# Moving tiles of the full blocks read as two halves by turns, with a matching change of token order in the stores

## Chip, cores, metric

One core of one Trainium2 chip runs the whole program. The metric is device time in microseconds, median of the runs. TensorE (PE) multiplies, VectorE (DVE), ScalarE (ACT) and GpSimd (POOL) work element by element, and SyncE (SP) issues the transfers.

## The reference, cut to what matters

```python
def mab(q, kv):                                  # attention, scale = 1 / sqrt(128)
    s = scale * (q @ kv.T); a = softmax(s); return a @ kv
h = mab(inducing, x)                             # 32 x 128 from 12480 tokens x 128
x = mab(x, h)                                    # 12480 x 128
def _moe_ref(x, w_in, w_out, s, b):              # d_ff = 2048
    r = np.maximum(x @ w_in, 0.0)
    return (s * (r * r) + b) @ w_out
def _moe2_ref(x, w_in, w_out):
    h = x @ w_in
    g = np.where(h >= 1, h, np.where(h <= -1, 0.0, (h + 1) ** 2 / 4))
    return g @ w_out
```

The inputs are float32, the weight matrices float64. The output is 12480 x 128 float32.

## The kernel before

The tokens are worked in 25 blocks: 24 full ones of 512 tokens (`TB`) and a short one of 192. Tokens lie along the free dimension, the 128 channels on the partitions. A first part reads `x`, transposes it into tiles `x0` to `x24`, computes the 32 x 128 attention result, and turns the float64 weights into float32 (`win`, `wo_s`) or into two halves, a rounded one and the rest (`half(name, 0)`, `half(name, 1)`).

Then two feed-forward layers run as one software pipeline. One step handles two of the 16 chunks of `d_ff` (`GW` = 2, `SPB` = 8 steps a block, 200 steps in all). Of step t, layer 1 does `in1` (product of the softmax weights `qt` with `hw`, two matmuls), `relu1`, `sq1`, `split1` and, two steps later, `out1`; layer 2 works `LAG` = 18 steps behind with `in2`, `clip2`, `sq2`, `g2`, `split2_hi`, `split2_lo` and, three steps later, `out2`. To keep precision at the speed of one pass, `in2`, `out1` and `out2` are each three matmuls per chunk: (rounded weight, rounded data), (rounded weight, rest of data), (rest of weight, rounded data), all of type F32R. With a full block each reads a moving tile of 128 x 512 four-byte words and writes one bank of 128 x 512 in PSUM. A steady step holds 2 + 6 + 6 + 6 = 20 of these one-pass matmuls. In the first 18 steps the product of layer 1 is `out1_whole`, plain float32, which the trace shows as two MATMUL records for one matmul; the last, short block ends with `out2_whole`, float32 too.

The order on each engine is fixed by the code: a planner (`Plan`) with estimated costs orders the first part, the first steps and the last ones, and the string `ORDER` the steps between: `in1 relu1 ev1 sq1 evh out2 in2 ev2 clip2 hi2- lo2- misc sq2 evl miscd split1 out1 g2`, where the minus means the step before. Layer 1 has one buffer for `h1` (two banks of PSUM), layer 2 two for `h2`; `y1` and `y2` are one bank each. So `in2` of a step waits for `lo2` of two steps before, which is the last reader of its buffer.

`store(bl)` reads the accumulated `y2` bank: DVE transposes it in 32 x 32 squares into a tile `o` (two buffers), and four transfers, one for each group of 32 channels, write it to the output in pieces of 32 floats. A block's tokens were loaded four to a partition, so column k*128 + p of a tile is token 4p + k, and the store's address pattern undoes that.

In the trace before, L661 is `in1`; L714, L715 and L716 are the three matmuls of `outp` (for `out1` and `out2` alike); L726 is `out1_whole`; L751 to L753 are `in2`; L795 is `out2_whole`; L758, L762, L769, L235 and L779 are `clip2`, `sq2`, `g2`, `split2_hi` and `split2_lo`; L674 and L681 `relu1` and `sq1`; L691 and L239 `split1`.

## Time and profile before

| what | value |
|---|---|
| three runs | 983.13, 985.3, 987.97 us, median 985.3 |
| the profiled execution | 984.17 us, of which the span (first to last instruction) is 982.4 us |
| PE busy | 959.7 us, 98% of the span |
| DVE, ACT, POOL busy | 805.0, 843.6, 753.3 us |
| granted TensorE clock, mean | 0.995 |
| DMA | 28.11 MB, most of it in the first 60 us |

The page gives busy times by engine, the span in 40 slices, the chain of work that ended last, and the costliest groups of instructions. A MATMUL's duration in it includes the time to drain, and the ends are modelled; the time that a stream of matmuls needs is therefore read from one start to the next in the timeline.

### The profile page before, as it was taken

The numbers are of one execution on the slowest core, as the hardware profiler recorded it, in microseconds if no ns is written. First come the engines' busy times: TensorE is split into PE (matmuls) and PEld (weight loads), VectorE is DVE, ScalarE is ACT, GpSimd is POOL, SyncE is SP. The second block draws the span as 40 slices with busy tenths as digits, with TensorE's granted clock in tenths as the row PEclk, the third lists the DMA queues.
The fourth block names the chain that finished last, engine by engine and source line by source line (L and its number), as shares of the span: only waits on it lengthen the run. The fifth ranks groups of instructions, "written<-read, shape, count | busy, mean of one in ns | idle before, by whom it ended". The sixth has DMA issues, their size and how long they took to land.

```text
span 982.4 us, 12391 instructions
## 1 busy us (share of the span) xinstructions
PE 959.7 (98%) x4492; PEld 770.0 (78%) x4492; DVE 805.0 (82%) x834; ACT 843.6 (86%) x910; POOL 753.3 (77%) x510
## 2 busy tenths in 40 slices
PE   5999999999999999999999999999999999999997
PEld 3754588888888888888888888888888888888776
DVE  6878788888888878888888888878888888888895
ACT  5748989989898988998898898998998899898774
POOL 0121379988899888899889898888898888887463
PEclk9989999999999999999999999999999999999999
DMA  8612000100002000002000002000001000000000
GB/s 322 218 31 78 0 1 12 44 11 12 4 7 54 11 1 12 11 0 54 12 1 11 11 0 55 12 1 11 11 1 43 12 1 11 16 1 11 11 12 15
DMA packets 65469, 28.11 MB, mean 29 GB/s; under 512 B 54016, under 2 KB 58368, under 8 KB 65408
## 3 DMA queue, kind: packets, MB, share of 16 engines
q1 hardware_dynamic: 65408, 27.33, 10.5%
q8 instruction: 35, 0.57, 0.2%
q14 instruction: 26, 0.21, 0.1%
HBM read 14.80 MB, written 6.39 MB: 22 GB/s over the span
## 4 chain that ended last, share of the span: by engine, by line
PE 93%; ACT 2%; DVE 2%; DMA 2%; issue 0%; DVEq 0%; ACTq 0%
PE y L714 17%; PE y L715 17%; PE y L716 17%; PE h L751 9%; PE h L753 9%; PE h L752 9%; PE h L661 9%; PE y L726 3%; DMA xc<-in_x_dram 1%; PE ptr L305 1%; DVE cl L758 1%; ACT g L681 1%; PE ph L378 1%; ACT g L674 1%; DVE lo L779 1%; PE pw L883 1%
## 5 line engine op out<-in xcount | busy, mean ns | idle before, releaser
L691 POOL TENSOR_TENSOR lo<-g,hi 128x1024 fp32r<-128x1024 f32 (+1 forms) x182 | 427.7, 2350 | 15.2
L758 DVE TENSOR_SCALAR cl<-h 128x1024 f32<-128x1024 f32 (+2 forms) x202 | 239.3, 1186 | 126.0 <-PE h L753 125.9
L762 ACT ACTIVATE cl<-cl,mhalf 128x1024 f32<-128x1024 f32 (+2 forms) x202 | 226.8, 1124 | 83.9 <-DVE cl L758 83.6
L714 PE MATMUL y<-hi,wout 128*128 128x512 f32 (+1 forms) x748 | 289.5, 387 | 0.9 <-DVE o L804 0.9
L715 PE MATMUL y<-lo,wout 128*128 128x512 f32 (+1 forms) x748 | 289.3, 387 | 0.0
L716 PE MATMUL y<-hi,wout 128*128 128x512 f32 (+1 forms) x748 | 289.2, 387 | 0.0
L239 POOL TENSOR_SCALAR hi<-g 128x1024 fp32r<-128x1024 f32 (+1 forms) x182 | 187.0, 1027 | 88.8 <-PE y L716 75.7
L769 DVE SCALAR_TENSOR_TENSOR h<-h,cl 128x1024 f32<-128x1024 f32 x182 | 223.2, 1226 | 13.9 <-ACT cl L762 2.7
L779 DVE TENSOR_TENSOR lo<-h,hi 128x1024 fp32r<-128x1024 f32 x182 | 221.6, 1217 | 3.0 <-ACT hi L235 0.5
L681 ACT ACTIVATE g<-g 128x1024 f32<-128x1024 f32 (+1 forms) x200 | 207.5, 1039 | 5.4
L674 ACT ACTIVATE g<-h 128x1024 f32<-128x1024 f32 (+1 forms) x197 | 194.2, 986 | 5.3 <-PE h L661 5.3
L235 ACT CAST hi<-h 128x1024 fp32r<-128x1024 f32 x182 | 181.7, 999 | 4.8 <-DVE h L769 4.8
L714 PEld LDWEIGHTS y<-hi,wout 128*128 128x128 f32 x748 | 140.5, 188 | 29.8 <-issue 1.3
L716 PEld LDWEIGHTS y<-hi,wout 128*128 128x128 f32 x748 | 140.4, 188 | 28.7
L715 PEld LDWEIGHTS y<-lo,wout 128*128 128x128 f32 x748 | 140.5, 188 | 28.3
L751 PE MATMUL h<-y,win 128*128 128x512 f32 (+1 forms) x400 | 154.8, 387 | 1.1 <-DVE lo L779 1.0
L752 PE MATMUL h<-y,win 128*128 128x512 f32 (+1 forms) x400 | 153.9, 385 | 0.0
L753 PE MATMUL h<-y,win 128*128 128x512 f32 (+1 forms) x400 | 153.8, 385 | 0.0
L661 PE MATMUL h<-qt,hw 128*128 128x512 f32 (+1 forms) x400 | 124.9, 396 | 0.7 <-ACT g L674 0.6
L661 PEld LDWEIGHTS h<-qt,hw 128*128 128x128 f32 x400 | 74.5, 188 | 22.8 <-issue 6.2
L751 PEld LDWEIGHTS h<-y,win 128*128 128x128 f32 x400 | 75.1, 188 | 17.8 <-DVE lo L779 2.0
L753 PEld LDWEIGHTS h<-y,win 128*128 128x128 f32 x400 | 75.2, 188 | 15.1
(139 smaller groups left out, 612.5 us busy)
## 6 DMA issues: line engine op xcount, KB each, us to landing
xc<-in_x_dram SPq DMA_DIRECT2D x24, 256.0 KB, 6.5
out_dram<-o SPq DMA_DIRECT2D x96, 64.0 KB, 2.2
qin<-x SPq DMA_DIRECT2D x92, 64.0 KB, 2.0
raw_in<-in_moe_w_in_dram SPq DMA_DIRECT2D x8, 512.0 KB, 5.6
raw_out<-in_moe_w_out_dram SPq DMA_DIRECT2D x8, 512.0 KB, 6.2
xc<-in_x_dram SPq DMA_DIRECT2D x1, 96.0 KB, 6.7
qin<-x SPq DMA_DIRECT2D x4, 24.0 KB, 2.7
out_dram<-o SPq DMA_DIRECT2D x4, 24.0 KB, 1.9
```

The source lines that it names most:

```text
L661: nc.tensor.matmul(p[:, j, :tb(bl)], hw[f // 4][:, (f % 4) * 128:(f % 4 + 1) * 128], qt[bl], start=True, stop=True)
L691: engine[eng].tensor_sub(lo1[t], g1.pop(t), hi1[t].bitcast(F32))
L714: nc.tensor.matmul(p, whi, hi[:, j, :], start=first, stop=False)
L715: nc.tensor.matmul(p, whi, lo[:, j, :], start=False, stop=False)
L716: nc.tensor.matmul(p, wlo, hi[:, j, :], start=False, stop=last)
L751: nc.tensor.matmul(p[:, j, :tb(bl)], whi, y1h[bl], start=True, stop=False)
L752: nc.tensor.matmul(p[:, j, :tb(bl)], wlo, y1h[bl], start=False, stop=False)
L753: nc.tensor.matmul(p[:, j, :tb(bl)], whi, y1l[bl], start=False, stop=True)
L758: nc.vector.tensor_scalar(cl[t][:, part(js)], h2[t][:, part(js), :tb(t // SPB)], -1.0, 1.0, op0=ALU.max, op1=ALU.min)
L762: nc.scalar.activation(k, k, AF.Square, bias=mhalf, scale=0.5)
L769: nc.vector.scalar_tensor_tensor(oo[t][:, part(js)], h, -1.0, cl[t][:, part(js)], op0=ALU.max, op1=ALU.add)
L779: engine[eng].tensor_sub(lo2[t][:, part(js)], oo[t][:, part(js)], hi2[t][:, part(js)].bitcast(F32))
```

## The change

Two helpers make views of a tile of a full block. `turns` reads it in the order 0, 256, 1, 257, ..., 255, 511: the first and the second half by turns, so neighbouring columns come from addresses 1024 bytes apart and each half is walked in sequence. `turned` describes the output with two inner elements that follow each other, so that the product's columns are written to PSUM in plain sequence. Column 2b + a of the output is thus token column 256a + b of the input.

This is done in `in1`, `outp` (`out1` and `out2`), `out1_whole` and `in2` for the 24 full blocks. The element-wise work between is unchanged: it does not mind which token a column is. Each of the four products on a token's way rotates the nine bits of the column number by one, four in all, and with the order from loading the store needs another address pattern. It is still four transfers a block, of 64 KB each, in pieces of 32 floats. The short block keeps its order; `out2_whole`, which serves it alone, is untouched. Neither the planner's costs nor the order of instructions on any engine changes: the two programs stand in the same order on PE, DVE, ACT, POOL and SP, and the only rows that differ in shape are the stores (outermost count 8 in place of 128).

```diff
+    def turns(v, bl):
+        return v.rearrange("p (a b) -> p b a", a=2) if tb(bl) == TB else v
+    def turned(v, bl):
+        return v.rearrange("p (b a) -> p b a", a=2) if tb(bl) == TB else v
...
-            nc.tensor.matmul(p[:, j, :tb(bl)], hw[f // 4][:, (f % 4) * 128:(f % 4 + 1) * 128], qt[bl],
-                             start=True, stop=True)
+            nc.tensor.matmul(turned(p[:, j, :tb(bl)], bl), hw[f // 4][:, (f % 4) * 128:(f % 4 + 1) * 128],
+                             turns(qt[bl], bl), start=True, stop=True)
...
-        p = p[:, :tb(t // SPB)]
+        bl = t // SPB
+        p = turned(p[:, :tb(bl)], bl)
         for j in js:
+            mhi, mlo = turns(hi[:, j, :], bl), turns(lo[:, j, :], bl)
...
-            nc.tensor.matmul(p, whi, hi[:, j, :], start=first, stop=False)
-            nc.tensor.matmul(p, whi, lo[:, j, :], start=False, stop=False)
-            nc.tensor.matmul(p, wlo, hi[:, j, :], start=False, stop=last)
+            nc.tensor.matmul(p, whi, mhi, start=first, stop=False)
+            nc.tensor.matmul(p, whi, mlo, start=False, stop=False)
+            nc.tensor.matmul(p, wlo, mhi, start=False, stop=last)
...
-            nc.tensor.matmul(acc1(bl)[:, :tb(bl)], wo_s[:, f, :], g[:, j, :], ...
+            nc.tensor.matmul(turned(acc1(bl)[:, :tb(bl)], bl), wo_s[:, f, :], turns(g[:, j, :], bl), ...
...
-            nc.tensor.matmul(p[:, j, :tb(bl)], whi, y1h[bl], start=True, stop=False)
-            nc.tensor.matmul(p[:, j, :tb(bl)], wlo, y1h[bl], start=False, stop=False)
-            nc.tensor.matmul(p[:, j, :tb(bl)], whi, y1l[bl], start=False, stop=True)
+            o, mhi, mlo = turned(p[:, j, :tb(bl)], bl), turns(y1h[bl], bl), turns(y1l[bl], bl)
+            nc.tensor.matmul(o, whi, mhi, start=True, stop=False)
+            nc.tensor.matmul(o, wlo, mhi, start=False, stop=False)
+            nc.tensor.matmul(o, whi, mlo, start=False, stop=True)
...
-        ov = out[t0:t0 + n].rearrange("(q t k) (r d) -> r t k q d", t=NM, k=kb, d=NM)
+        if n == TB:
+            ov = out[t0:t0 + n].rearrange("(q s u) (r d) -> r u q s d", q=KB, u=2 * KB, d=NM)
+        else:
+            ov = out[t0:t0 + n].rearrange("(q t k) (r d) -> r t k q d", t=NM, k=kb, d=NM)
+            o = o.rearrange("p (k q) d -> p k q d", k=kb)
         for r in range(C // NM):
-            nc.sync.dma_start(out=ov[r], in_=o[NM * r:NM * (r + 1)].rearrange("p (k q) d -> p k q d", k=kb))
+            nc.sync.dma_start(out=ov[r], in_=o[NM * r:NM * (r + 1)])
```

## Rows read from the trace of the kernel before

**Rows 1.** The page: busy us, share and instructions; then the chain that ended last.

```profile
PE 959.7 (98%) x4492; PEld 770.0 (78%) x4492; DVE 805.0 (82%) x834; ACT 843.6 (86%) x910; POOL 753.3 (77%) x510
PE 93%; ACT 2%; DVE 2%; DMA 2%; issue 0%; DVEq 0%; ACTq 0%
```

**Rows 2.** Windows: stretch, busy us (instructions) of PE, PEld, DVE, ACT, POOL; clock, DMA.

```profile
60.00:130.00 70.00, 68.02 (x250) 35.51 (x248) 56.74 (x86) 58.37 (x66) 21.05 (x18) 1.00 0.14 38
...
567.00:676.00 109.00, 109.00 (x482) 90.26 (x481) 90.36 (x81) 98.84 (x101) 95.66 (x63) 1.00 0.08 18
...
894.00:950.00 56.00, 54.95 (x268) 44.88 (x266) 49.73 (x43) 42.66 (x51) 31.26 (x30) 1.00 0.03 6
950.00:983.00 33.00, 26.26 (x147) 22.87 (x146) 21.32 (x33) 16.06 (x20) 15.50 (x7) 0.95 0.11 20
```

**Rows 3.** Timeline of PE in a steady step: start, length, instruction.

```profile
500.16 0.62 PE L661 MATMUL h<-qt,hw 128*128 128x512 f32 x2
500.61 0.39 PE L714 MATMUL y<-hi,wout 128*128 128x512 f32 x1
...
504.69 0.61 PE L661 MATMUL h<-qt,hw 128*128 128x512 f32 x2
```

**Rows 4.** Groups of PE by line and shape, the whole span: counts and mean.

```profile
L714 PE MATMUL y<-hi,wout 128*128 128x512 f32 x732 | 285.3, 390 | 0.9 <-DVE o L804 0.9
L751 PE MATMUL h<-y,win 128*128 128x512 f32 x384 | 150.1, 391 | 1.1 <-DVE lo L779 1.0
L661 PE MATMUL h<-qt,hw 128*128 128x512 f32 x384 | 122.0, 401 | 0.7 <-ACT g L674 0.6
L726 PE MATMUL y<-g,wo_s 128*128 128x512 f32 x72 | 33.9, 607 | 1.2 <-ACT g L681 0.7 <-ACT y1f L730 0.4
```

**Rows 5.** Timeline of PE: plain float32 records, of 512 and of 192 columns.

```profile
79.15 4.03 PE L726 MATMUL y<-g,wo_s 128*128 128x512 f32 x9
...
969.50 1.46 PE L795 MATMUL y<-g,x 128*128 128x192 f32 x8
```

**Rows 6.** Timeline of PE after a short product has broken the stream.

```profile
903.46 0.36 PE L661 MATMUL h<-qt,hw 128*128 128x192 f32 x2
903.66 0.42 PE L714 MATMUL y<-hi,wout 128*128 128x512 f32 x1
903.92 0.40 PE L715 MATMUL y<-lo,wout 128*128 128x512 f32 x1
904.16 0.39 PE L716 MATMUL y<-hi,wout 128*128 128x512 f32 x1
...
905.77 0.40 PE L751 MATMUL h<-y,win 128*128 128x512 f32 x1
```

**Rows 7.** Timeline of PE: one-pass products of 192 columns, the first with weights ready.

```profile
961.98 0.25 PE L751 MATMUL h<-y,win 128*128 128x192 f32 x1
962.06 0.28 PE L752 MATMUL h<-y,win 128*128 128x192 f32 x1
```

**Rows 8.** Groups of DVE, whole span: one reads every second word, one reads neighbours.

```profile
L448 DVE SCALAR_TENSOR_TENSOR cva_in<-raw_in,cvs_in 128x512 uint32<-128x512 uint32 x8 | 5.5, 691 | 0.3
L468 DVE TENSOR_TENSOR wout<-cva_out,wout 128x512 fp32r<-128x512 f32 x4 | 2.7, 686 | 0.1
```

**Rows 9.** Timeline of two steps, a block's turn first: DVE, ACT, PE's weight loads.

```profile
332.61 1.23 DVE L779 TENSOR_TENSOR lo<-h,hi 128x1024 fp32r<-128x1024 f32 x1
334.01 0.19 PEld L751 LDWEIGHTS h<-y,win 128*128 128x128 f32 x1
...
500.14 1.22 DVE L779 TENSOR_TENSOR lo<-h,hi 128x1024 fp32r<-128x1024 f32 x1
500.26 1.16 ACT L762 ACTIVATE cl<-cl,mhalf 128x1024 f32<-128x1024 f32 x1 [0.47 <-DVE cl L758]
501.75 0.19 PEld L751 LDWEIGHTS h<-y,win 128*128 128x128 f32 x1
503.53 1.23 DVE L758 TENSOR_SCALAR cl<-h 128x1024 f32<-128x1024 f32 x1 [0.85 <-PE h L753]
```

**Rows 10.** The page's DMA issues: stores, KB each, us to landing.

```profile
out_dram<-o SPq DMA_DIRECT2D x96, 64.0 KB, 2.2
```

## The prediction

> **What bounds the kernel now.** I read the page first: PE is busy 98% of the span, and 93% of the chain that ended last is PE [rows 1]. [...]

> Then the pace itself. A step is 20 one-pass matmuls of 512 columns, and from one `in1` to the next pass 504.69 - 500.16 = 4.53 us, so **one takes 0.2265 us**; I use 226.7 ns [rows 3]. [...] So the one-pass matmul pays some **12 ns that half a two-pass record does not** (226.7 against 214.6; unrounded the record is 429.2).

> [...] The surplus isn't constant: after a short product has broken the stream, the same matmul takes 0.26, 0.24, 0.22 us and so on, nine in 2.11 us, before the 226.7 come back [rows 6]; it depends on how things fall in time. [...] And it is there whether DVE or ACT work or not, since all 20 matmuls of a step take the same. I read this as a cost of fetching the moving words (or of fetching them beside the next weights), near a limit of that path. No row shows which.

> **The change, part by part.**

> *The reading order.* The affected one-pass matmuls are 3 x 732 + 3 x 384 + 384 = 3732 (L715 and L716 count like L714, L752 and L753 like L751) [rows 4]. None of the trace's matmuls reads its moving tile other than in plain sequence, so the price must be bounded. [...] From above: if a fetch brings only neighbours and a column that isn't next to the last costs a fetch of its own, the nearest row is the pace at which the float32 record takes new columns, 429 ns for 512, a loss of 202 ns each. [...] The nearest row for reading that isn't in sequence is on another engine: DVE takes 691 ns for two operands of which one is every second word, and 686 for two in sequence [rows 8], so there a skip alone costs nothing; but two neighbours there are 8 bytes apart and here 1024. I take 214.6: each half is walked in sequence, at half the pace, and a path that is short by one part in eighteen at full pace and not short at all at half pace needs little relief. That is a choice, not a row, and the two-fold price stays as a rival.

> [...]

> *The sum for the stream.* 764 us x 12.1/226.7 = 40.8 us saved if nothing else becomes late.

> *The ends.* From 60 to 130 us PE handles only 250 records in 68 us [rows 2], and the one-pass ones among them, 36 of `in1` and two dozen of layer 2, mostly stand between waits for ACT: at most 60 x 12 ns = 0.7 us, I take 0.3. From 894 to 983 us some 300 one-pass products of 512 columns run, 3.6 us at the full gain; but the chain there goes through pieces of DVE and ACT as well, and PE is idle 1.05 us in one window and 6.7 in the other [rows 2]. I take 2.0. The 72 float32 records of `out1_whole` [rows 4] are now read by turns too; they ask for words at half the pace and have no surplus, so neither gain nor, at the two-fold price, loss: 0.

> *What becomes late.* At 214.6 a step is 4.29 us. ACT's 98.84 us of 109 become 98.84 of 103.2, 96%; POOL 93%, DVE 88%. So no engine passes PE, but the slack of the tightest wait shrinks. `in2`'s weights are loaded when `lo2` of two steps before is done; its end and that load are 501.75 - 501.36 = 0.39 us apart in an ordinary step, and 334.01 - 333.84 = 0.17 at a block's turn, where `evac1` has delayed ACT and so `hi2` [rows 9]. Between the two `in2` stand 14 other matmuls, 14 x 12.1 = 0.17 us less. So an ordinary step keeps 0.22, and a turn has nothing left; the load itself leads its matmul by 0.22 us, which covers it. A wait of up to 0.05 us at each of 23 turns is 1.1 us; I put 1.0 us back.

> *The stores.* 96 transfers of 64 KB, landed after 2.2 us [rows 10], keep their number and pieces; their addresses are other. A block comes every 36 us and `o` has two buffers, so even ten times the landing time is hidden; the last store of a full block has some 30 us of the short block behind it, and the very last is unchanged. SP has nothing else due then. Cost 0, with that cover; without it, the landing time once. DVE's transposes and all other element-wise work are the same instructions on the same tiles: 0.

> **The sum**: 40.8 + 0.3 + 2.0 - 1.0 = 42.1 us off the profiled execution's own 984.2 us is 942.1. That execution is 1.1 us under the median of the three runs, 985.3, so I forecast **943 us**. [...]

> **The rivals.**

> 1. *The order of reading is not what costs.* If the 12 ns come from the weights' reads beside the moving ones, or from anything that counts words and not places, every matmul stays at 226.7 and the time at 985, within 980 to 990. For it: the surplus moves with timing [rows 6]. Against: the float32 records load weights too, without a surplus.

> 2. *The stream never locks.* The spacings after a break [rows 6] show that the same work can cost 231 to 234 ns. If reading by turns keeps PE in that state, 3370 matmuls of the stream (764/0.2267) cost 4.6 to 7.8 ns more, 15 to 26 us: 1000 to 1012. It is slower from the point where a matmul passes 228 ns.

> 3. *Each column becomes a fetch of its own.* Place: the moving reads of all 3732 matmuls; price: up to 202 ns each, as bounded above. The stream becomes 764 x 429/226.7 = 1446 us, 682 more; the last part some 250 x 0.2 = 50 more, the ramp about 10: 1.73 ms. It decides from the point where such fetches come slower than the 0.443 ns a column of now (226.7/512). For it: the one-pass read has no room now. Against: the DVE rows, and that the neighbours of a word are needed only two columns later.

> **How the numbers follow.** My forecast (a gain of 25 to 49 us, 936 to 960) gets 0.50, rival 1 0.16, rival 2 0.14, rival 3 0.20. Half a per cent (5 us) is about what a measurement of this kernel can tell from no change. Faster by more: the forecast, 0.50. Within: rival 1, with the smallest losses, 0.17. Slower: rivals 2 and 3, 0.33. 213.3 ns a matmul and no new waits would save 764 x 13.4/226.7 = 45.2 us, with the ends 47.5, and end at 938; the range starts at 935, since runs of one kernel scatter by 2 to 3 us (983.1 to 988.0), and reaches over rivals 1 and 2 to 1012; rival 3, 0.20, is left out. Faster cases alone: 935 to 960.

> **What would show it.** Right: in a steady step the distance between two `in1` is 4.29 us, the float32 records stay at 429 ns, DVE's wait for `in2` falls from 0.85 to about 0.6 us, and PE is idle for hundredths of a microsecond at most before `in2` at a block's turn. Rival 1: 4.53 us again. Rival 2: 4.62 to 4.68. Rival 3: 8.6 us, with the float32 records still at 429 (if these double too, fetches are costlier than I bounded). The step most in doubt is the price of the reading order; if it is right and the total isn't, the loss is in the waits for `lo2`, or in ACT at 96%.

## The result, and the profile after

The changed kernel takes **955.47 us** (median of four runs, 954.44 to 955.68) where the kernel before took 984.47 beside it: ratio 0.9698, 95% interval 0.9671 to 0.9725. It is faster by 29 us; the forecast was 943, 42 us faster. The profiled execution is the one of 954.44 us, its span 952.7 us against 982.4.

The first thing to see is the pace of the steady stream. Windows of the changed kernel (stretch, busy us and instructions of PE, PEld, DVE, ACT, POOL, granted clock, DMA), which answer to [rows 2]:

```profile
60.00:130.00 70.00, 67.83 (x224) 30.82 (x224) 51.38 (x81) 52.48 (x60) 15.98 (x14) 1.00 0.14 38
...
567.00:676.00 109.00, 109.00 (x505) 94.56 (x504) 93.94 (x83) 102.71 (x105) 98.64 (x66) 1.00 0.09 18
```

In the same 109 us there are 505 matmuls where there were 482, at the same granted clock, and ACT is busy 94%. In the ramp it is the other way: 224 matmuls in 70 us where there were 250. Two starts of `in1` in the timeline of PE (start, length, instruction), against [rows 3]:

```profile
507.44 0.59 PE L669 MATMUL h<-qt,hw 128*128 128x512 f32 x2
...
511.76 0.59 PE L669 MATMUL h<-qt,hw 128*128 128x512 f32 x2
```

A step is 4.32 us by these rounded starts; **a one-pass matmul takes 215.7 ns in place of 226.7** (109 us/505 is 215.8). What the ramp (the first 18 steps, up to the start of the steady stream) lost shows on the float32 products of layer 1 (shortest, median and longest duration in ns, first and last start in us; first the kernel before, then the changed one):

```profile
L726 PE MATMUL y<-g,wo_s x72: 591/592/697, 66.9 to 115.2; 128*128 128x512 f32 x72
...
L661 PE MATMUL h<-qt,hw x400: 249/389/799, 63.9 to 925.4; 128*128 128x512 f32 x128, 128*128 128x192 f32 x6
...
L736 PE MATMUL y<-g,wo_s x72: 700/703/805, 67.3 to 122.3; 128*128 128x512 f32 x72
...
L669 PE MATMUL h<-qt,hw x400: 254/379/892, 64.4 to 896.5; 128*128 128x512 f32 x128, 128*128 128x192 f32 x6
```

Their median rose from 592 ns to 703, and the last of them starts at 122.3 us where it started at 115.2. The last `in1` starts at 896.5 where it started at 925.4. So the ramp ends 7.1 us later, the stretch from there to the last `in1` is 36.0 us shorter, and the rest, up to the end of the span, 0.8 us shorter: together the 29.7 us of the span.

Last the waits of the stream, from 130 to 866 us (engine, line waited for: us in total, times, longest):

```profile
DVE cl L769 <- PE h L764: 78.9, 145, 0.6
...
ACT cl L773 <- DVE cl L769: 34.7, 132, 0.5
...
PEld h L762 <- DVE lo L790: 4.6, 22, 0.2
PEld y L724 <- issue: 3.8, 21, 0.2
```

The last two are new: PE's weight loads wait once a block for `lo2`, and once for something that the view leaves without a name ("issue"). Both stand in one turn of a block, on the timeline of ACT, PE's weight loads and DVE:

```profile
327.55 0.77 ACT L740 ACTIVATE y1f<-y,bcol,s_sb 128x512 f32<-128x512 f32 x1
...
328.39 0.19 PEld L724 LDWEIGHTS y<-hi,wout 128*128 128x128 f32 x1 [0.18 <-issue]
...
329.17 1.01 ACT L235 CAST hi<-h 128x1024 fp32r<-128x1024 f32 x1
...
330.21 1.22 DVE L790 TENSOR_TENSOR lo<-h,hi 128x1024 fp32r<-128x1024 f32 x1 [0.33 <-ACT hi L235]
...
331.49 0.19 PEld L762 LDWEIGHTS h<-y,win 128*128 128x128 f32 x1 [0.21 <-DVE lo L790]
```

The evacuation on ACT ends at 328.32 and `out1` of the next block, which writes the same bank, loads its weights at 328.39. The same 0.77 us make `hi2` late, `lo2` after it (DVE waits 0.33), and `in2`'s weights after that. The loads lead their matmuls by 0.21 us (median of the stretch from 130 to 860 us), so PE itself loses only 0.045 us (a distance of 0.261 between two starts in place of 0.216) and 0.076 (0.292); over the stretch from 130 to 860 us these distances add up to 2.6 us.

### The profile page after: what moved, and what is told of

Read it like the earlier page. It is cut to its first block, busy times and chain, and to the rows that moved or that the text cites. A ratio compares the mean times of both kernels' runs of the same rounds, so it can differ in the third digit from the quotient of the medians.

```text
span 952.7 us, 12390 instructions
## 1 busy us (share of the span) xinstructions
PE 929.2 (98%) x4492; PEld 772.5 (81%) x4492; DVE 805.3 (85%) x834; ACT 841.4 (88%) x910; POOL 745.7 (78%) x510
## 4 chain that ended last, share of the span: by engine, by line
PE 92%; DVE 3%; ACT 2%; DMA 2%; issue 1%; DVEq 0%; ACTq 0%
PE y L724 16%; PE y L725 16%; PE y L726 16%; PE h L762 9%; PE h L669 8%; PE h L764 8%; PE h L763 8%; PE y L736 4%; DMA xc<-in_x_dram 1%; DVE cl L769 1%; PE ptr L305 1%; ACT cl L773 1%; PE ph L378 1%; DVE lo L790 1%; PE pw L898 1%
## 5 line engine op out<-in xcount | busy, mean ns | idle before, releaser
L699 POOL TENSOR_TENSOR lo<-g,hi 128x1024 fp32r<-128x1024 f32 (+1 forms) x182 | 422.9, 2324 | 15.2
L724 PE MATMUL y<-hi,wout 128*128 128x512 f32 (+1 forms) x748 | 283.1, 378 | 1.4 <-DVE o L815 1.4
L725 PE MATMUL y<-lo,wout 128*128 128x512 f32 (+1 forms) x748 | 281.9, 377 | 0.0
L726 PE MATMUL y<-hi,wout 128*128 128x512 f32 (+1 forms) x748 | 281.8, 377 | 0.0
L724 PEld LDWEIGHTS y<-hi,wout 128*128 128x128 f32 x748 | 141.4, 189 | 24.4 <-issue 5.6
L726 PEld LDWEIGHTS y<-hi,wout 128*128 128x128 f32 x748 | 141.5, 189 | 19.5
L762 PE MATMUL h<-y,win 128*128 128x512 f32 (+1 forms) x400 | 152.6, 381 | 1.7 <-DVE lo L790 1.6
L764 PE MATMUL h<-y,win 128*128 128x512 f32 (+1 forms) x400 | 150.0, 375 | 0.0
L763 PE MATMUL h<-y,win 128*128 128x512 f32 (+1 forms) x400 | 149.9, 375 | 0.0
L669 PE MATMUL h<-qt,hw 128*128 128x512 f32 (+1 forms) x400 | 121.8, 389 | 0.7 <-ACT g L682 0.7
L762 PEld LDWEIGHTS h<-y,win 128*128 128x128 f32 x400 | 75.6, 189 | 18.3 <-DVE lo L790 7.0
L764 PEld LDWEIGHTS h<-y,win 128*128 128x128 f32 x400 | 75.7, 189 | 10.3
```

Source lines behind the costliest of these rows:

```text
L669: nc.tensor.matmul(turned(p[:, j, :tb(bl)], bl), hw[f // 4][:, (f % 4) * 128:(f % 4 + 1) * 128], turns(qt[bl], bl), start=True, stop=True)
L699: engine[eng].tensor_sub(lo1[t], g1.pop(t), hi1[t].bitcast(F32))
L724: nc.tensor.matmul(p, whi, mhi, start=first, stop=False)
L725: nc.tensor.matmul(p, whi, mlo, start=False, stop=False)
L726: nc.tensor.matmul(p, wlo, mhi, start=False, stop=last)
L762: nc.tensor.matmul(o, whi, mhi, start=True, stop=False)
```

## The experiments

**Reading orders by themselves.** To the kernel before I added groups of 24 equal products (12 of float32, two records each) behind the last work, all on one tile, so that nothing else runs beside them. This is one run.

```diff
+    m, o = y1h[NB - 2], pt[:, 0, :]          # 128 x 512 words in SBUF; one bank of PSUM
+    nc.tensor.matmul(o, wr(i), m, ...)                                             # L1184, plain
+    nc.tensor.matmul(seq2(o), wr(i), half2(m), ...)                                # L1186, halves by turns
+    ... m.rearrange("p (a b) -> p b a", a=4)                                       # L1188, quarters by turns
+    ... m.rearrange("p (b a) -> p a b", a=2)                                       # L1190, evens, then odds
+    ... m.rearrange("p (b a) -> p a b", a=4)                                       # L1192, every fourth word
+    ... m.rearrange("p (a b c) -> p b a c", a=2, c=2)                              # L1194, halves, two words each
+    ... m.rearrange("p (a b c) -> p b a c", a=2, c=4)                              # L1196, halves, four words each
+    ... m.rearrange("p (b a c) -> p b c a", a=2, c=4)                              # L1198, order 0,4,1,5,2,6,3,7
+    nc.tensor.matmul(o[:64], wr(i, 64), m, ...)                                    # L1200, 64 weight columns, plain
+    nc.tensor.matmul(o[:32], wr(i, 32), m, ...)                                    # L1202, 32 weight columns, plain
+    # L1206, L1208, L1210: float32: plain; halves by turns; plain, written to every second word
```

> The kernel before, with sixteen groups of 12 or 24 extra products behind its last work, all from one moving tile of 128 x 512 in SBUF into one bank of PSUM (their results are not used), each group with its own reading order or weight width. Theory A (the surplus comes from fetching the moving words in plain sequence at one word a column): plain order 226.7 ns from start to start, the same with 64 or 32 weight columns; halves by turns 215.7; quarters by turns (a new place at every column) about 216 as well; halves by turns in pairs or in fours in between, 216 to 227; evens then odds (every second word) open, 216 to 240. Theory B (the surplus comes from the next weights' reads beside the moving ones): plain order falls with the weight columns, to about 221 with 64 and 218 with 32; halves by turns is 216 whatever the weights. Theory C (each column away from its neighbour is a fetch of its own, which the one-pass product of the changed kernel has only just room for): every fourth word and quarters by turns cost far more, 400 ns. Float32, two records for a product: plain 429 ns a record, halves by turns 540 as in the changed kernel; read in plain order and written to every second word of PSUM: 429 if the reading is what costs there, 540 or more if stepping in PSUM costs as much.

The timeline of PE in that run (start, length, instruction, count):

```profile
979.55 5.79 PE L1184 MATMUL probe<-y,win 128*128 128x512 f32 x24
985.17 5.34 PE L1186 MATMUL probe<-y,win 128*128 128x512 f32 x24
990.35 6.96 PE L1188 MATMUL probe<-y,win 128*128 128x512 f32 x24
997.14 11.00 PE L1190 MATMUL probe<-y,win 128*128 128x512 f32 x24
1007.96 11.25 PE L1192 MATMUL probe<-y,win 128*128 128x512 f32 x24
1019.03 8.19 PE L1194 MATMUL probe<-y,win 128*128 128x512 f32 x24
1027.04 6.17 PE L1196 MATMUL probe<-y,win 128*128 128x512 f32 x24
1033.05 5.35 PE L1198 MATMUL probe<-y,win 128*128 128x512 f32 x24
1038.23 5.69 PE L1200 MATMUL probe<-y,win 128*64 128x512 f32 x24
1043.76 5.72 PE L1202 MATMUL probe<-y,win 128*32 128x512 f32 x24
...
1054.49 10.46 PE L1206 MATMUL probe<-y,win 128*128 128x512 f32 x24
1064.79 13.12 PE L1208 MATMUL probe<-y,win 128*128 128x512 f32 x24
1077.75 10.46 PE L1210 MATMUL probe<-y,win 128*128 128x512 f32 x24
```

From the start of one row to the next, over 24, a product costs: plain 234 ns (227 in most pairs; the first ten vary, 224 to 236, after a longer one), halves by turns **216**, quarters 283, evens then odds 451, every fourth word 461, halves in twos 334, halves in fours 250, and 0,4,1,5 216. Fewer weight columns change nothing in the plain order (230 and 232, with 64 and 32): **theory B falls**, the surplus does not shrink with the weights. Theory A holds for plain and halves, but it missed quarters and evens-then-odds (451, where it gave 240 at most), and halves in twos and in fours are slower than either end that I gave. Theory C is near with every fourth word (461 for 400) and misses quarters (283 for 400): a product that changes place at every column can even be the fastest (216). Float32 reads 429 ns a record in plain order ((10.46 - 0.59)/23), 540 by turns ((13.12 - 0.70)/23), and the same 429 when only the writing is stepped.

These numbers made a new theory, D, an inference from the times alone: the time goes as if the even and the odd columns were fetched as two streams side by side, each of which wants to take its words in sequence from lines of four words. Halves by turns gives each stream four words in a row from a line, plain gives it two, evens-then-odds one. Four is inferred from the steps within a stream: of one word 216 ns, of two 227, and of four and eight nearly the same, 451 and 461.

**Ten orders chosen against theory D.** Same arrangement, on a tile of 1024 words (`both`) and on its first half (`m`).

```diff
+    ... both.rearrange("p (a b) -> p b a", a=2)[:, :256, :]              # L1185, first 256 of each half
+    ... both.rearrange("p (a b s) -> p b a s", a=2, s=2)[:, :, :, 0]     # L1187, two places, every second word
+    ... both.rearrange("p (a b s) -> p b a s", a=2, s=4)[:, :, :, 0]     # L1189, every fourth, 256 columns
+    ... m.rearrange("p (b a c) -> p b c a", a=2, c=2)                    # L1191, order 0,2,1,3
+    ... m.rearrange("p (b a c) -> p b c a", a=2, c=8)                    # L1193, order 0,8,1,9
+    ... m.rearrange("p (a b c) -> p b a c", a=2, c=8)                    # L1195, halves, eight words each
+    ... m.rearrange("p (b a c) -> p b c a", a=2, c=128)                  # L1197, places 128 words apart
+    ... m.rearrange("p (a c b) -> p b c a", a=2, c=2)                    # L1199, quarters in another order
+    ... m[:, :256].unsqueeze(2).to_broadcast([128, 256, 2])              # L1201, order 0,0,1,1
+    ... m                                                                # L1203, plain
```

> The kernel before, with ten groups of 24 extra one-pass products behind its last work (results unused), all with 128 x 128 weights. Theory D, formed from the first probes: the even and the odd columns of a product are fetched as two streams side by side, and each stream wants its next words from the 16 bytes it is at: four words in a row from one such line cost nothing (215.8 ns), two in a row 227, one 451, and going back and forth between lines costs extra. Theory E: only the number of places that the whole sequence visits by turns counts, two being best (216), one 227, four 283, whatever the words. From a tile of 1024 words: two places by turns, each in sequence (first 256 of each half): D and E 216. Two places by turns, each taking every second word: D 227, E 216. Two places by turns, each taking every fourth word, 256 columns: D 225, E 112 (the weight loads' pace). From 512 words: order 0,2,1,3 in each four: D 227 (both streams take two words of a line in a row), E about 227 or 216. Order 0,8,1,9 in each sixteen: D and E 216. Runs of eight from two halves by turns: D between 227 and 250, E as well. Two places 128 words apart by turns, in two stretches: both 216. Quarters as (first, second), (third, fourth), so that each stream goes back and forth between two places: D 283 as with quarters by turns, E 283. Each word twice (0,0,1,1): D 216, E 227, since one place. Plain: 227.

```profile
979.65 2.75 PE L1185 MATMUL probe<-y,win 128*128 128x512 f32 x12
982.24 5.62 PE L1187 MATMUL probe<-y,win 128*128 128x512 f32 x24
987.70 5.68 PE L1189 MATMUL probe<-y,win 128*128 128x256 f32 x24
993.20 5.63 PE L1191 MATMUL probe<-y,win 128*128 128x512 f32 x24
998.67 5.34 PE L1193 MATMUL probe<-y,win 128*128 128x512 f32 x24
1003.85 6.00 PE L1195 MATMUL probe<-y,win 128*128 128x512 f32 x24
1009.69 5.34 PE L1197 MATMUL probe<-y,win 128*128 128x512 f32 x24
1014.87 6.72 PE L1199 MATMUL probe<-y,win 128*128 128x512 f32 x24
1021.43 5.34 PE L1201 MATMUL probe<-y,win 128*128 128x512 f32 x24
1026.61 5.63 PE L1203 MATMUL probe<-y,win 128*128 128x512 f32 x24
```

**Float32 in plain order.** The ramp's 7 us, tried in the changed kernel: the reading is undone and the turn done on the writing side.

```diff
-            nc.tensor.matmul(turned(acc1(bl)[:, :tb(bl)], bl), wo_s[:, f, :], turns(g[:, j, :], bl), ...)
+            o, m = acc1(bl)[:, :tb(bl)].rearrange("p (b a) -> p a b", a=2), g[:, j, :].rearrange("p (a b) -> p a b", a=2)
+            nc.tensor.matmul(o, wo_s[:, f, :], m, ...)
```

> The changed kernel, but the float32 products of layer 1 in the first 18 steps read their moving tile in plain sequence and write every second word of PSUM instead, so that tokens stand where they stood. My theory: their 540 ns a record, 111 more than before, come from reading by turns and cost the ramp the 7 us by which it is later; 429 again, 72 x 0.111 = 8 us at most off, of which 6 to 8 reach the end: 947.5 to 949.5. Rival: those 7 us are lost to something else in the ramp (waits for ACT), then the records go back to 429 but the time stays within 2 us of 955.5. Second rival: writing every second word costs as much, then the records stay at 540 or above and the time at 955 or later.

948.65 us (947.86 to 950.38), ratio 0.9637 [0.9619, 0.9655] to the kernel before, 6 to 7 us under the changed kernel by ratio and by median. Its float32 products (same columns as above):

```profile
L737 PE MATMUL y<-g,wo_s x72: 592/592/697, 67.4 to 115.5; 128*128 128x512 f32 x72
```

592 ns again, and the last at 115.5. The ramp's loss is those 72 records read by turns.

**One product undone.** In the changed kernel `in2` reads plainly; the tokens of a full block come out in another order.

```diff
-            o, mhi, mlo = turned(p[:, j, :tb(bl)], bl), turns(y1h[bl], bl), turns(y1l[bl], bl)
+            o, mhi, mlo = p[:, j, :tb(bl)], y1h[bl], y1l[bl]
```

> The changed kernel with one part undone: the three products of in2 read in plain sequence, the other products by turns; the tokens of a full block therefore come out in another order (the stores are left as they are). If the price belongs to each product's own reading: in2's products 226.7 ns from start to start, the others 215.7, 384 x 3 x 0.011 = 12.7 us more, 968. If it is a matter of how the stream as a whole falls in time: all products at one pace between, and in2 not singled out.

966.85 us, one run, 11 over the changed kernel's median (expected 12.7). In the timeline `out2` (L724 to L726), then `in2` (L762 to L764), then `out1`:

```profile
500.34 0.38 PE L724 MATMUL y<-hi,wout 128*128 128x512 f32 x1
...
501.63 0.40 PE L762 MATMUL h<-y,win 128*128 128x512 f32 x1
501.87 0.39 PE L763 MATMUL h<-y,win 128*128 128x512 f32 x1
...
503.00 0.38 PE L724 MATMUL y<-hi,wout 128*128 128x512 f32 x1
```

Six by turns take 1.29 us, 215 ns each; six plain ones 1.37, 228 each. The price belongs to each product's own reading.

**The waits at a block's turn.** Three runs. The first, on the changed kernel, moves two steps in the order of the work:

```diff
-ORDER = "in1 relu1 ev1 sq1 evh out2 in2 ev2 clip2 hi2- lo2- misc sq2 evl miscd split1 out1 g2"
+ORDER = "in1 ev1 relu1 evh out2 in2 ev2 clip2 hi2- lo2- misc sq1 sq2 evl miscd split1 out1 g2"
```

> The changed kernel with another order of the work in a step: the evacuation of layer 1's bank comes ahead of relu1 on ACT, and sq1 behind hi2 of the step before. At a block's turn of the changed kernel out1's first weights wait 0.18 us for that evacuation and in2's 0.21 us for lo2, which lets the matmuls behind them start 0.045 and 0.076 us late. My theory: both waits go, 22 x 0.12 = 2.6 us, 953. Rival: sq1 comes later, so POOL's split1 and then out1 wait instead; the time rises by more than that, over 956.

958.83 us (958.46 to 961.46), ratio 0.9741 [0.9724, 0.9758]: 3 to 4 us slower than the changed kernel. It is the rival's time, but not the whole of its reason. The waits, 130 to 866 us:

```profile
DVE h L780 <- ACT cl L773: 78.2, 145, 1.0
ACT hi L235 <- DVE h L780: 57.6, 148, 0.7
POOL hi L239 <- ACT g L689: 44.0, 73, 0.8
...
PEld h L762 <- DVE lo L790: 8.4, 22, 0.7
PE h L762 <- DVE lo L790: 1.5, 6, 0.3
PEld y L724 <- issue: 1.2, 5, 0.3
```

`split1` on POOL does wait for `sq1`, as the rival says, but no wait of `out1` follows from it. `out1`'s wait nearly goes (21 times to 5), but without `sq1` between, `hi2` now waits for `g2` and `g2` for `sq2`, in most steps, and `in2` waits longer for `lo2`. By the distances of PE's starts (130 to 860 us) the turns now cost 5.8 us where they cost 2.6, 5.3 of it at `in2`. That `sq1` had filled a gap is my reading. So the next run, on the kernel with float32 in plain order, leaves it:

```diff
+ORDER = "in1 ev1 relu1 sq1 evh out2 in2 ev2 clip2 hi2- lo2- misc sq2 evl miscd split1 out1 g2"
```

> The changed kernel with the plain reading of the float32 products and the evacuation on ACT ahead of relu1, sq1 left where it was. The wait of out1's weights for the evacuation goes, 22 x 0.045 = 1.0 us; lo2 is as late as before, so that wait stays: 947.7. If, as in the run where sq1 was moved too, the time rises, the early evacuation is what did it; if it falls, sq1's place did.

950.90 us (950.48 to 954.08), ratio 0.9657 [0.9640, 0.9674]: about 2 us slower, where 1.0 faster was expected; the two intervals overlap, but each of its four runs lies above the other kernel's four. `out1`'s wait is gone, `in2`'s has grown (the waits, 130 to 860 us; then PE at one turn):

```profile
PEld h L763 <- DVE lo L791: 8.4, 22, 0.4
...
325.61 0.38 PE L726 MATMUL y<-hi,wout 128*128 128x512 f32 x1
325.97 0.48 PE L763 MATMUL h<-y,win 128*128 128x512 f32 x1
...
326.29 0.38 PE L764 MATMUL h<-y,win 128*128 128x512 f32 x1
```

The evacuation still stands ahead of `hi2` on ACT, and `in2`, no longer held back by `out1`, is due earlier. The wait of its weights, 0.39 us at this turn, is now longer than the 0.2 us by which a load leads its matmul: the first product of `in2` starts 0.15 us late and the second 0.10 later still (0.36 and 0.32 us in place of 0.216). From 130 to 860 us the turns cost PE 5.4 us, against 2.6 with the evacuation where it was; the difference of 2.8 us is about the loss. The last run takes the 0.77 us off ACT, on the same kernel, and puts the evacuation one step earlier in the order, right behind the `out1` that it reads:

```diff
+        if eng == "DVE":
+            nc.vector.tensor_scalar(y1f[bl], y1p.pop(bl)[:, :tb(bl)], s_sb, bcol, op0=ALU.mult, op1=ALU.add)
...
-ORDER = "in1 relu1 ev1 sq1 evh out2 in2 ev2 clip2 hi2- lo2- misc sq2 evl miscd split1 out1 g2"
+ORDER = "in1 relu1 sq1 evh out2 in2 ev2 clip2 hi2- lo2- misc sq2 evl miscd split1 out1 ev1 g2"
...
-                d = a - D1 - (1 if name == "ev1" else EVD)
+                d = a - D1 - (0 if name == "ev1" else EVD)
```

> The changed kernel with the plain reading of the float32 products, and in the steps between ramp and tail the evacuation of layer 1's bank by DVE, ahead of g2, in place of ACT. My theory of the two waits at a block's turn (out1's weights for the evacuation, in2's for lo2, behind them 0.045 and 0.076 us of PE): both go, because ACT has 0.77 us less there and DVE, with 0.5 us idle a step, catches up in the step after; 22 x 0.12 = 2.6 us less than 948.65: 946. Rival: DVE is late by the evacuation's 0.7 us where lo2 is due, and in2 waits longer than before: 949 to 955.

**945.51 us** (944.54 to 946.65), ratio 0.9592 [0.9576, 0.9608], 3 to 4 us under the kernel with float32 in plain order, and the fastest of all. Engine and place changed together, so which of the two it takes is not shown. Of the waits of its stream, 130 to 860 us, one is left on PE's side, the last line:

```profile
DVE cl L773 <- PE h L768: 67.3, 122, 0.6
ACT cl L777 <- DVE cl L773: 41.3, 153, 0.5
...
PEld h L766 <- DVE lo L794: 0.2, 1, 0.2
```

## Why the prediction was right, and where it was off

- **The bound**: right. PE sets the pace before and after; the gain came out of it at 11 ns a matmul. The 764 us of the sum are the stretch from 130 to 894 us of the kernel before: PE is busy for 764.00 of them at a granted clock of 1.00, ACT for 692.35, POOL 677.04, DVE 633.44. The step came at 4.32 us where 4.29 was named as a sign, and DVE's wait for `in2` is 0.6 us at the longest, as named. That 955 lies in the range says little, since 935 to 1012 would have held a slower kernel too.
- **The price of the reading order**: the direction and nearly the size. 215.7 ns came where I took 214.6; over the 764 us that is 764 x 11.0/226.7 = 37.1 us and not 40.8. That the 214.6, half of the 429.2 ns from one float32 record to the next [rows 5], is one passage of the columns without a surplus was an estimate, and no run shows it. No run shows the 213.3 ns either, from which 45.2 us, 938 and so the lower end of the range are worked out: in its place the changed kernel has spacings of 215 to 217 ns in nearly every pair from 130 to 860 us, and none shorter. The choice of 214.6 over the two-fold price rested on an argument and no row, and it could have gone the other way: every second word, which costs DVE nothing [rows 8], costs TensorE twice the time (451). No run shows the reason given, relief for a path that is short at full pace: "each half walked in sequence, at half the pace" would also let quarters by turns be fast, and they are the slower for it (283). The times fit better with the sequence that the even and the odd columns each see, though the price of quarters does not follow from that either.
- **The float32 records at 0**: wrong, and the largest miss. They take 540 ns by turns, 72 x 0.111 = 8.0 us, 7.1 of them at the end of the ramp. I had argued from their pace, half of the other's (429 ns a record against 226.7), that they had room; I gave no bound above zero, though no row showed them read in any other order. Their 429 was named as a sign of being right, and it failed. They were the one operation of the change whose price I set without two ends. Why turns cost them time is open.
- **What becomes late**: the right wait at the right place (`lo2` at a block's turn), 0.076 us of PE each where I allowed 0.05. I did not see the second, `out1` behind the evacuation, 0.045 us. Together 22 x 0.12 = 2.6 us where I put 1.0.
- **The ends**: 2.0 us expected from 894 us on and 0.3 in the ramp's one-pass products. Not measured by themselves; what is left of the 29.7 us of the span when the other terms are taken out is as much, 29.7 + 7.1 - 37.1 + 2.6 = 2.3, of which 0.8 came behind the last `in1`.
- **Stores and element-wise work at 0**: no wait for either is in the waits of the stream, and no run tried the stores by themselves.
- The shortfall of 12.4 us (42.1 against 29.7 of the span) is thus 7.1 in the ramp, 3.7 in the rate and 1.6 at the turns, 12.4 together.
- **Rivals**: 1 fell (226.7 is gone), 2 fell (the spacing is 215 to 217 in nearly every pair), and 3 is true of other orders and not of this one (evens then odds 451, every fourth word 461, above the 429 that I had as the upper end).

## What to carry to other kernels

Where one-pass float32 products of 512 columns set the pace and start 227 ns apart, let the even and the odd columns each read their words in sequence, from two places by turns (216 here), and keep PSUM in sequence; the token order can be mended once, in the store. Price every operation that a new access pattern touches, also those with a slower pace: leave float32 products in plain order and turn them on the writing side (here 429 ns a record, against 540 when read by turns). When a bound is shortened by 5%, look at the turn of the outer loop, where one extra step (here 0.77 us on ACT, the busiest engine but PE) takes the slack first.

## What the runs showed of the hardware

- A one-pass product of 512 columns costs 216 ns from start to start where even and odd columns each take four words in a row, 227 to 229 with two, 451 to 461 with one. Where a stream goes back and forth between two places the price lies between (halves in twos 334, fours 250, eights 243; quarters 283 and 273), and no rule found here gives it. The distance made no difference: 4, 8, 128, 256 and 512 words apart by turns are all 216.
- The weights' width made no difference to it in plain order: 227 ns with 128 columns in most pairs, 230 with 64, 232 with 32.
- A plain float32 record of 512 columns costs 429 ns in sequence and 540 with halves by turns, the opposite sign.
- Writing a float32 product to every second word of PSUM cost no time: 429 ns a record, as in sequence. For one-pass products it was not measured.
- The unsteady spacings after a break [rows 6] were seen in the plain order: by turns the spacing is back at 215 to 217 ns in the next pair after a wait (changed kernel, 130 to 860 us), while plain `in2` behind other products by turns has spacings of 0.22 to 0.24 us.
